# Attention, then routed experts: a 512-column copy ahead of two row copies, six row tiles, one weight load issued later

## The chip, the cores and the metric

The kernel runs on one core of one Trainium2 chip. The metric is device time in microseconds (us). Five engines work beside each other, each through its own instruction stream in order: PE (matrix products), DVE, ACT and POOL (element work), and SP, which here only issues DMA transfers. PE, DVE, ACT and POOL wait for each other and for transfers by semaphores.

## The reference

```python
scores = scale * np.matmul(q, k.transpose(0, 1, 3, 2))      # q, k, v: (8, 12, 448, 64)
scores = np.where(mask, -1000000000.0, scores)              # causal
attn = np.exp(scores - np.max(scores, axis=-1, keepdims=True))
attn = attn / (np.sum(attn, axis=-1, keepdims=True) + 1e-09)
x = np.matmul(attn, v)                                      # reordered to (3584, 768)
...
logits = x @ w_gate                                         # 8 experts
expert_idx = np.argmax(logits, axis=1)
gate_w = probs[np.arange(N), expert_idx]
for e in range(E):                                          # at most 80 tokens each, by largest gate_w
    h = np.maximum(x[tok_idx] @ w1[e], 0.0)                 # w1: (8, 768, 1024), w2: (8, 1024, 768)
    out[tok_idx] = gate_w[tok_idx, None] * (h @ w2[e])
```

Tokens that no expert keeps give rows of zeros.

## The kernel before

**Attention.** The eight batches go one after the other, each as six pairs of heads. Each pair passes through scores (PE), masked row minima (DVE), exponentials (ACT), transposes (PE) and products with v (PE). Between these stand, by a table of due times, the steps of the batch before: its gate, its choice of 80 tokens for each expert so far, and the writing of its rows of x to a DRAM buffer `xs`.

**The tail.** The last batch has nothing behind it to hide in. Its steps are issued in the order of a string of names, `TAIL` (L37 to L42), which a loop at the end of the manual schedule walks through. Each name issues one step, on the engine that the step uses. In a name `rNw` is the transpose of row group N by PE (L566) and `rNe` its scaling and its store: `ROW_ENGINES` gives r0 to DVE (L581), r1 to r3 to ACT (L576, one instruction per head), and r4 to r7 to ACT and POOL (a copy out of PSUM by ACT, L578, then a product in place by POOL, L579). Each `rNe` ends with a store of the row tile `xr` into `xs`, issued by SP (L582). Row groups 3 and 7 have 64 rows, the others 128.

**The choice.** `r0t` and `r1t` transpose two tables on PE (L676) and `r0c` and `r1c` copy them from PSUM into `ex` (L679): `r0c` on DVE the one-hot rows, `r1c` on ACT the three 16-bit parts of the gate weights. `rl`, `lt`, `cp`, `ro` compare the earlier batches' table with the new weights. `c3w` to `c0w` are products of the two halves of `ex` on PE (L690), `c3l` to `c0l` the comparisons on DVE (L693). From them come the ranks, the moves into the table (`rr`, `tn`, `tab`), and at the end `idx`, the rows of `xs` that each expert reads (L838). `*6`, `*2`, `*5` and `*18` issue that many products of no use (`wp`, L1010), which keep PE at work.

**The experts.** The first gather (L1098, on POOL, an indirect DMA) reads expert 0's rows out of `xs`. By its semaphores it waits for the landing of every row store and for `idx`. POOL then writes one column of a `wl` tile (L1228), for which DVE's first weight split (L1066) waits. Weights come as 32 pieces of 1536 KB, split by ACT (L1081) and DVE (L1066) into two 16-bit halves. There are ten buffers for pieces (`wraw`). Nine loads are issued before the tail's choice begins; the name `piece` in `TAIL` issues the tenth, into space that `close` frees. The eleventh has to wait until the first buffer is free again, which needs the splits.

Row tiles `xr` come from a pool with a fixed number of buffers in turn; a row group that takes a buffer waits until the store that last read it has landed. The loads and stores named here are all issued by SP, on one queue.

Of the kernel before, what the change touches and what calls it, by code (L numbers as in the profile page):

```python
# [7 lines left out]
F32 = mybir.dt.float32  # L8
# [9 lines left out]
P = 128  # L18
# [16 lines left out]
LATE = 23  # L35

TAIL = """  # L37
u ta ya rest rest tb yb v0 td yd tc yc v1 vy guard invert last_rows w gp0 wy close piece rest rest gp1 gs
r0w r0e lp r1w r1e r2w r3w r4w r5w *6 lg logit shifted chosen r2e r3e sums one_hot weight weighted columns parts
r0t r0c r1t rl lt r4e r5e r1c r6w r7w cp ro r6e c3w c3l r7e c2w c2l c1w c1l c0w c0l  # L40
*2 gt places earlier own *5 rank rr tn tab *18
"""  # L42
ROW_ENGINES = "vaaapppp"
# [3 lines left out]
def attention_then_moe(  # L47
# [32 lines left out]
    spool = sel_stack.enter_context(tc.tile_pool(name="sel", bufs=2, side="right"))  # L80
# [11 lines left out]
    def bank(shape, dtype, name):  # L92
        return (ps_x or ps_m).tile(shape, dtype, name=name, tag="x" if ps_x else "misc")
# [51 lines left out]
    def whole_tile(t):  # L145

        return slice(queries(t).start, queries(t).start + P)
# [329 lines left out]
    NH = NP // 2  # L477
# [29 lines left out]
    def norm_of(bt, t, hs, m):  # L507
        return bt.rl[0:m, hs] if t == NO else bt.sums[0:m, t * H + hs.start:t * H + hs.stop]
# [40 lines left out]
    def row_group(bt, t, g, how="v"):  # L549

        b = bt.b
        m = min(P, S - t * P)
        got = []

        def turn():
            if ps_x:

                own = len(row_banks) % 2
                tp = (ps_t if own else ps_m).tile([P, NH, P], F32, name="rt", tag="tp" if own else "misc",
                                                  padded_shape=[P, 4, P])  # L560
                row_banks.append(tp)
            else:
                tp = bank([P, NH, P], F32, "rt")
            got.append(tp)
            for i in range(NH):
                nc.tensor.transpose(tp[:, i, :], bt.xu[:, g * NH + i, whole_tile(t)], ident)  # L566

        def store():
            tp = got[0]
            xr = spool.tile([P, NH * P], F32, name="xr", tag="xr", bufs=4)  # L570
            src = tp[0:m].rearrange("k p (j d) -> k (p j) d", d=DH)
            dst = xr[0:m].rearrange("k (h d) -> k h d", d=DH)
            norm = norm_of(bt, t, slice(g * 2 * NH, (g + 1) * 2 * NH), m)
            if how == "a":
                for i in range(2 * NH):
                    nc.scalar.mul(dst[:, i, :], src[:, i, :], norm[:, i:i + 1])  # L576
            elif how == "p":
                nc.scalar.copy(dst, src)  # L578
                nc.gpsimd.tensor_tensor(out=dst, in0=dst, in1=norm.unsqueeze(2).to_broadcast([m, 2 * NH, DH]), op=ALU.mult)  # L579
            else:  # L580
                nc.vector.tensor_tensor(out=dst, in0=src, in1=norm.unsqueeze(2).to_broadcast([m, 2 * NH, DH]), op=ALU.mult)  # L581
            nc.sync.dma_start(xs[b * S + t * P:b * S + t * P + m, g * NH * P:(g + 1) * NH * P], xr[0:m, :])  # L582
        return [turn, store]
# [311 lines left out]
    with tc.manual_schedule():  # L895
# [79 lines left out]
        rest = [f for k in sorted(plan) for f in plan.pop(k)]  # L975
# [226 lines left out]
    for s in range(NSL):  # L1202
# [4 lines left out]
        for e in range(E):  # L1207
            u = Unit()
# [8 lines left out]
        with tc.manual_schedule(engines={mybir.EngineType.PE}):  # L1217
            for e in range(E + 1):
                if e < E:
                    u = units[e]  # L1220
# [70 lines left out]
```

## Time and profile before

| | us |
|---|---|
| median of 3 runs | 495.69 |
| lowest and highest | 493.9, 499.05 |
| the profiled execution's own time | 493.27 |
| its span, first to last instruction | 491.6 |
| mean granted clock of PE, share of full | 0.991 |

The span is 1.67 us shorter than the profiled execution's time, which holds the start and the end around it. The attention part fills about 0 to 344 us of the span, the tail of the last batch about 344 to 372 us and the experts the rest. A row of a timeline gives the start, the duration, the engine, the line and the tiles written and read; what stands in brackets is how long the engine was idle ahead of it and what ended the wait.

### The profile page before, as it was taken

How to read it: one execution, taken by the hardware profiler on the slowest of the kernel's cores; microseconds unless marked ns; L12 is line 12 of the kernel's file. 1: busy time of each engine (PE TensorE's matmuls, PEld its weight loads, DVE VectorE, ACT ScalarE, POOL GpSimd, SP SyncE). 2: the span in 40 equal slices, each digit the busy share in tenths (PEclk: the TensorE clock that was granted, in tenths of full speed). 3: DMA queues.
4: the chain of work that ended last, by engine and by line, in shares of the span. 5: the costliest groups of instructions: out<-in, count | busy, mean ns of one | idle time of the engine just before them, and what ended most of it. 6: DMA issues, size and time to landing. Idle time of an engine off the chain costs nothing. (4 is left out here: it accounts for less than half of the span.)

```text
span 491.6 us, 14840 instructions
## 1 busy us (share of the span) xinstructions
PE 447.9 (91%) x5282; PEld 343.1 (70%) x5282; DVE 427.8 (87%) x1297; ACT 419.4 (85%) x1089; POOL 270.6 (55%) x343
## 2 busy tenths in 40 slices
PE   3899989999999999999999999999979999989885
PEld 1566656756766675676667567677538999989885
DVE  5787879979988997998999799899568999999982
ACT  5999989979997997999799799988485999989881
POOL 6788786565668665566866556580136155511001
PEclk9999999999999999999999999999979999999999
DMA  7777996899579579856957985539936999999921
GB/s 217 198 186 190 275 274 189 249 264 285 148 214 269 147 231 253 259 148 215 262 153 227 270 240 157 187 119 328 418 137 201 372 387 387 391 423 424 421 81 41
DMA packets 49145, 120.88 MB, mean 246 GB/s; under 512 B 6146, under 2 KB 33026, under 8 KB 45616
## 3 DMA queue, kind: packets, MB, share of 16 engines
q1 hardware_dynamic: 47856, 116.21, 73.5%
q0 software_dynamic: 1056, 3.51, 2.3%
q8 instruction: 41, 0.67, 0.6%
q10 hardware_dynamic: 160, 0.23, 0.2%
q14 instruction: 32, 0.26, 0.2%
HBM read 96.36 MB, written 23.99 MB: 245 GB/s over the span
## 5 line engine op out<-in xcount | busy, mean ns | idle before, releaser
L421 ACT ACTIVATE prob<-ns,nb 128x128 f32<-128x128 f32 (+3 forms) x336 | 176.8, 528 | 20.5 <-DVE nb L418 19.0
L418 DVE CUSTOM_DVE_ANT_0 ns<-sp,mask 128x384 f32<-128x384 f32 (+2 forms) x288 | 116.2, 415 | 24.3 <-PE sp L397 10.7
L438 PE MATMUL tp<-ident,prob 128*128 128x128 f32 x768 | 121.5, 278 | 8.0 <-ACT prob L421 6.9
L438 PEld LDWEIGHTS tp<-ident,prob 128*128 128x128 f32 x768 | 88.5, 142 | 26.0 <-ACT prob L421 14.3
L1066 DVE SCALAR_TENSOR_TENSOR wl<-wraw,wh 128x768 f16<-128x768 f32 (+1 forms) x98 | 97.7, 1061 | 4.2 <-ACT wh L1081 2.4
L372 POOL TENSOR_TENSOR qk<-qk,qk 128x448 f16<-128x448 f32 x94 | 97.4, 1056 | 5.9 <-DVE qk L364 2.8
L450 ACT COPY PT<-tp 128x512 f32<-128x512 f32 x144 | 82.4, 572 | 16.3 <-PE sp L396 13.0
L367 POOL TENSOR_TENSOR qk<-qk,qk 64x448 f16<-64x448 f32 x47 | 49.3, 1049 | 81.3 <-ACT qk L360 45.2
L468 PE MATMUL xp<-PT,vt 128*64 128x448 f32 (+3 forms) x768 | 91.3, 380 | 0.0
L1081 ACT ACTIVATE wh<-wraw 128x768 f16<-128x768 f32 (+1 forms) x98 | 84.3, 924 | 2.4 <-PE hp L1141 1.7
L396 PE MATMUL sp<-qk 128*128 128x384 f16 (+2 forms) x288 | 75.9, 278 | 9.0 <-ACT qk L349 5.6
L468 PEld LDWEIGHTS xp<-PT,vt 128*64 128x64 f32 x768 | 54.9, 137 | 41.6 <-issue 22.4
L397 PE MATMUL sp<-qk 128*128 128x384 f16 (+2 forms) x288 | 78.0, 276 | 0.8 <-DVE qk L348 0.8
L1138 PEld LDWEIGHTS <-wh 128*128 128x128 f16 x668 | 67.2, 101 | 2.6 <-issue 2.6
L1140 PEld LDWEIGHTS <-wh 128*128 128x128 f16 x668 | 66.7, 100 | 2.0 <-issue 2.0
L1141 PEld LDWEIGHTS <-wl 128*128 128x128 f16 x668 | 66.7, 100 | 0.2 <-issue 0.2
L421 ACT ACTIVATION_READ_ACCUMULATOR prob<-ns,nb 128x1 f32 x336 | 63.8, 190 | 0.0
L1195 POOL DMA_INDIRECT out<-yo,idx x8 | 22.8, 2844 | 66.9 <-ACT yo L1192 61.8
L368 POOL TENSOR_TENSOR qk<-qk,qk 64x448 f16<-64x448 f32 x47 | 48.9, 1040 | 3.5
L1141 PE MATMUL op<-hh,wl 128*128 128x80 f16 x348 | 38.9, 202 | 1.3 <-issue 1.3
L396 PEld LDWEIGHTS <-qk 128*128 128x128 f16 x288 | 28.5, 99 | 15.8 <-issue 6.5
L1140 PE MATMUL op<-hl,wh 128*128 128x80 f16 x348 | 38.9, 202 | 0.6 <-issue 0.6
(173 smaller groups left out, 910.1 us busy)
## 6 DMA issues: line engine op xcount, KB each, us to landing
wraw<-w SPq DMA_DIRECT2D x27, 1536.0 KB, 15.6
qk<-k_t SPq DMA_DIRECT2D x92, 224.0 KB, 5.0
out<-mask_l SPq DMA_DIRECT2D x56, 192.0 KB, 3.9
qk<-q_t SPq DMA_DIRECT2D x23, 448.0 KB, 3.4
vt<-v_t SPq DMA_DIRECT2D x24, 384.0 KB, 5.8
xs<-xr SPq DMA_DIRECT2D x48, 192.0 KB, 3.3
wraw<-w SPq DMA_DIRECT2D x24, 256.0 KB, 5.6
vt<-v_t SPq DMA_DIRECT2D x24, 64.0 KB, 5.5
```

The lines of the kernel that those rows point to most:

```text
L372: nc.gpsimd.tensor_tensor(out=k_lo[j][:, i], in0=kf[j][:, i], in1=k_hi[j][:, i], op=ALU.subtract)
L396: nc.tensor.matmul(sp[:, 0:w], qx[:, p, t * P:w], kx[:, p, 0:w], start=True, stop=False)
L397: nc.tensor.matmul(sp[:, 0:w], qx[:, p, t * P:w], lx[:, p, 0:w], start=False, stop=True)
L418: pr.masked = nc.vector.tensor_tensor_reduce(out=ns[:, 0:w], in0=sp[:, 0:w], in1=m, scale=-1.0 / 8.0, scalar=HUGE, op0=ALU.add, op1=ALU.mi ...
L421: nc.scalar.activation(pr.P[:, off:off + w], ns[:, 0:w], AF.Exp, bias=nb, scale=-1.0, accum_out=total)
L438: nc.tensor.transpose(pr.tp[:, i], pr.P[:, off:off + P], ident)
L450: copy(dst, src)
L468: state["pe"] = nc.tensor.matmul(xp[rows, 0:w], st["vt"][:, c, p * P + j * DH:p * P + (j + 1) * DH], pr.PT[:, j, n0:n0 + w], start=(c == 0 ...
L1066: return nc.vector.scalar_tensor_tensor(out=l, in0=src, scalar=SW, in1=h, op0=ALU.mult, op1=ALU.subtract)
L1081: nc.scalar.activation(h, src, AF.Copy, scale=SW)
L1140: nc.tensor.matmul(o, wh[:, ws], al[:, c, :], start=False, stop=False, skip_group_check=True)
L1141: nc.tensor.matmul(o, wl[:, ws], ah[:, c, :], start=False, stop=(x == n - 1), skip_group_check=True)
```

## The change

Three things change. In `TAIL`, `r1c` moves from behind `r5e` to ahead of `r4e`, and `piece` moves from behind `close` to behind `r5e`. The row tiles `xr` get six buffers for four.

```diff
 TAIL = """
-u ta ya rest rest tb yb v0 td yd tc yc v1 vy guard invert last_rows w gp0 wy close piece rest rest gp1 gs
+u ta ya rest rest tb yb v0 td yd tc yc v1 vy guard invert last_rows w gp0 wy close rest rest gp1 gs
 r0w r0e lp r1w r1e r2w r3w r4w r5w *6 lg logit shifted chosen r2e r3e sums one_hot weight weighted columns parts
-r0t r0c r1t rl lt r4e r5e r1c r6w r7w cp ro r6e c3w c3l r7e c2w c2l c1w c1l c0w c0l
+r0t r0c r1t rl lt r1c r4e r5e piece r6w r7w cp ro r6e c3w c3l r7e c2w c2l c1w c1l c0w c0l
...
-            xr = spool.tile([P, NH * P], F32, name="xr", tag="xr", bufs=4)
+            xr = spool.tile([P, NH * P], F32, name="xr", tag="xr", bufs=6)
```

On ACT, in the tail, from r2e (L576) to the first split of weights (L1081), the difference of the two orders:

```order
 L576 ACTIVATE xr<-rt,sums 128x64 x6
 L576 ACTIVATE xr<-rt,rql 64x64 x6
-L578 COPY xr<-rt 128x384 x2
 L679 COPY ex<-selt 24x512
-L578 COPY xr<-rt 128x384
+L578 COPY xr<-rt 128x384 x3
 L578 COPY xr<-rt 64x384
 L1081 ACTIVATE wh<-wraw 128x1024 x8
```

The copy of the gate parts (L679) now stands directly behind r3e, and the copies of r4 to r7 (L578) follow it without a break.

On SP, from the last row store of the batch before to the loads of the experts part (`wraw<-w` is a weight piece, `xs<-xr` a row store, `out<-mask_l` a store of zeros):

```order
 L582 DMA xs<-xr 64x384
 L301 DMA out<-mask_l 128x384
-L196 DMA wraw<-w 128x3072 x2
+L196 DMA wraw<-w 128x3072
 L582 DMA xs<-xr 128x384 x3
 L582 DMA xs<-xr 64x384
-L582 DMA xs<-xr 128x384 x3
+L582 DMA xs<-xr 128x384 x2
+L196 DMA wraw<-w 128x3072
+L582 DMA xs<-xr 128x384
 L582 DMA xs<-xr 64x384
 L196 DMA wraw<-w 128x3072 x22
```

Of the two pieces that stood ahead of all eight row stores one stays; the other is now behind the stores of r0 to r5 and ahead of those of r6 and r7. On PE, DVE and POOL the order is the same.

## Rows read from the trace of the kernel before

**Rows 1.** The page's head: the span, and each engine's busy time.

```profile
span 491.6 us, 14840 instructions
...
PE 447.9 (91%) x5282; PEld 343.1 (70%) x5282; DVE 427.8 (87%) x1297; ACT 419.4 (85%) x1089; POOL 270.6 (55%) x343
```

**Rows 2.** Windows: stretch, length, busy (PE, PEld, DVE, ACT, POOL), clock, DMA, GB/s.

```profile
364.00:370.00 6.00, 5.68 (x35) 2.88 (x36) 3.09 (x15) 6.00 (x7) 1.37 (x4) 0.50 0.16 50
...
430.00:440.00 10.00, 8.57 (x203) 8.34 (x200) 10.00 (x14) 8.06 (x14) 2.28 (x1) 1.00 1.01 424
```

**Rows 3.** Timeline of POOL: start, length, engine, line, operation [idle before <- releaser].

```profile
360.96 2.40 POOL L579 TENSOR_TENSOR xr<-xr,sums 128x384 f32<-128x384 f32 x3 [4.02 <-ACT xr L578]
...
368.58 1.08 POOL L1098 DMA_INDIRECT xg<-xs,idx  x1 [4.44 <-DVE gws L843]
369.68 0.11 POOL L1228 MEMSET wl<- 128x1 f16 x1
```

**Rows 4.** Timeline of DVE, from the rank counts to the first expert.

```profile
359.84 0.22 DVE L724 TENSOR_SCALAR ro<-cp,pnum 80x8 f16<-80x8 f32 x1 [0.29 <-PE cp L719]
362.28 0.75 DVE L693 SCALAR_TENSOR_TENSOR less<-rn,ggw,before 128x512 bf16<-128x512 f32 x1 [2.22 <-PE rn L690]
...
367.61 0.16 DVE L838 TENSOR_TENSOR idx<-xf,tn 80x8 int32<-80x8 f32 x1
...
369.82 3.50 DVE L1066 SCALAR_TENSOR_TENSOR wl<-wraw,wh 128x1024 f16<-128x1024 f32 x3 [1.57 <-POOL wl L1228]
...
380.02 0.66 DVE L1117 SCALAR_TENSOR_TENSOR xl<-xtp,xh 128x480 f16<-128x480 f32 x1
```

**Rows 5.** Timeline of ACT around the copy of the gate parts.

```profile
356.99 1.31 ACT L576 ACTIVATE xr<-rt,rql 64x64 f32<-64x64 f32 x6
360.41 0.94 ACT L578 COPY xr<-rt 128x384 f32<-128x384 f32 x2 [2.10 <-DMA xs<-xr]
361.25 0.57 ACT L679 COPY ex<-selt 24x512 bf16<-24x512 bf16 x1
```

**Rows 6.** Timeline of PE, from the keep-warm products to the first expert.

```profile
355.78 1.30 PE L1010 MATMUL wp<-before,identb 128*128 128x448 bf16 x6
...
357.98 0.38 PE L676 MATMUL selt<-identb,mv 128*128 128x128 bf16 x4 [0.34 <-DVE mv L665]
...
359.05 0.75 PE L719 MATMUL cp<-oh,lt 128*80 128x8 bf16 x4
361.87 0.65 PE L690 MATMUL rn<-ex 128*128 128x512 bf16 x3 [2.07 <-ACT ex L679]
...
367.23 5.04 PE L1010 MATMUL wp<-before,identb 128*128 128x448 bf16 x18
372.11 0.58 PE L1112 MATMUL xtp<-ident,xg 80*128 80x80 f32 x6
...
378.62 0.58 PE L1112 MATMUL xtp<-ident,xg 80*128 80x80 f32 x6
```

**Rows 7.** Timeline of SP's DMA queue, the whole stretch.

```profile
344.36 4.24 SPq L196 DMA_DIRECT2D wraw<-w  x2
353.52 11.10 SPq L582 DMA_DIRECT2D xs<-xr  x8
373.34 0.34 SPq L196 DMA_DIRECT2D wraw<-w  x1
```

**Rows 8.** DMA issues (KB, us to landing): pieces nine, ten, r0, r4, piece eleven.

```profile
wraw<-w SPq DMA_DIRECT2D x1, 1536.0 KB, 11.8
...
wraw<-w SPq DMA_DIRECT2D x1, 1536.0 KB, 11.5
...
xs<-xr SPq DMA_DIRECT2D x1, 192.0 KB, 6.8
...
xs<-xr SPq DMA_DIRECT2D x1, 192.0 KB, 1.9
...
wraw<-w SPq DMA_DIRECT2D x1, 1536.0 KB, 9.8
```

## The prediction

> **What bounds the kernel now.** Read the page first [rows 1]: PE, DVE and ACT are each busy over 85% of the span, which is an average over stages and decides nothing here. The windows tell the stages apart [rows 2]: while the experts run, DVE is busy 10.00 of 10.00 us and the DMA engines 1.01 of their time, so that part is full and moves as a block with its start; at 364 to 370 us PE is granted half its clock and DVE is busy 3.09 of 6.00 us, so the tail waits. Then the timelines, backwards from the experts. DVE's first weight split starts at 369.82 [rows 4], released by a memset that POOL issues right behind the first gather, and the gather starts at 368.58 after 4.44 us of waiting [rows 3]. It needs `idx`, which DVE ends at 367.61 + 0.16 = 367.77 [rows 4], and the landing of all row stores. SP's last store is issued by 353.52 + 11.10 = 364.62 [rows 7] and one such store lands in 1.9 [rows 8], so by 366.5: today `idx` is the later one, and the gather follows its end by 0.81.
>
> `idx` in turn hangs on a stop. PE has done the second table's transposes at 357.98 + 0.38 = 358.36 [rows 6], but ACT copies them into `ex` only at 361.25 [rows 5]: ahead of that copy stand r4e and r5e, and r4e waits 2.10 us for the landing of a row store, r0's, whose tile it takes with four buffers. PE then stands idle 2.07 us until `ex` [rows 6], and DVE waits 2.22 us for PE [rows 4].
>
> **Term 1, the copy ahead of the row groups.** ACT is free at 356.99 + 1.31 = 358.30 and the transposes end at 358.36, so the copy of 0.57 runs at about 358.4 and ends at 359.0 [rows 5, 6]. The products of L690 stand on PE behind `cp`, which ends at 359.80 for want of DVE's earlier work, so they start there, 2.07 earlier than 361.87 [rows 6]. DVE's first comparison follows the products' start by 362.28 - 361.87 = 0.41 and `ro`, which ends at 360.06: it starts at 360.2, 2.1 earlier [rows 4, 6]. All steps from there to `idx` are a chain of DVE and PE with nothing else in it, so `idx` ends at 365.7, and by `idx` alone the gather would start at 366.5. PE would also lose the idle time ahead of its fall to half clock, which I put at nothing on this chain, since its products there are short.
>
> **Term 2, six row tiles.** With six, r4e and r5e take tiles of older batches and wait for nothing; r6e and r7e take those of r0 and r1. The 2.10 wait [rows 5] goes. Two copies by ACT take 0.94 [rows 5], so r4 to r7 are copied from 358.9 to 360.8 and the splits of weights behind them start earlier by some 2 (358.4 for 360.41), which is worth nothing by itself: DVE's splits wait for POOL, not for them [rows 4]. POOL's product starts 360.96 - 360.41 = 0.55 behind ACT's copy and takes 2.40 / 3 = 0.80 [rows 3, 5]: r4 ends at 360.25, r5 at 361.05, r6 at 361.85, r7 at 362.65. Without term 3, all would have landed at 362.7 + 1.9 = 364.6, ahead of `idx`. In exchange r6e waits for r0's store. That one lands today at 353.52 + 6.8 = 360.3 [rows 7, 8], behind the tenth piece; with that piece gone from there it is 3.6 earlier (next term), so r6e at 359.8 finds it done.
>
> **Term 3, the tenth piece behind r5.** What a piece does to stores behind it is in the DMA issues. Piece nine is issued at 344.36 and lands in 11.8, at 356.2. Piece ten's issue ends at 344.36 + 4.24 = 348.60, and an issue takes 0.34, so it starts at 348.26 and lands in 11.5, at 359.8: 3.6 behind the other [rows 7, 8]. r0, issued at 353.52, lands at 360.3, 0.5 behind piece ten, although a store alone takes 1.9 [rows 8]. SP's transfers land in the order of their issue. So 3.6 is what a piece costs the stores behind it.
>
> Now the piece is issued when r5's store is: 361.05, and 0.34 later, say 361.4. Only r6 and r7 are behind it, but the gather needs both. The piece's landing is bounded by rows. Lowest: stores pass it, and it costs nothing. Highest: piece eleven, whose issue also finds its queue empty but meets the gathers, takes 9.8 [rows 8]. I take the stores' own time less the 0.5 that it adds behind another, 1.9 - 0.5 = 1.4, plus 3.6: 5.0, because at 361.4 nothing else but row stores is under way. The piece lands at 366.4, r6 at 366.9, r7 with half the rows at 367.2. The gather starts, with the same 0.81, at 368.0 and not at 366.5. Against 368.58 that leaves 0.6 of the 2.1.
>
> The piece itself is not missed: it is the last of ten loads and is read by the second layer of the second expert, after all of the first expert's work; DVE has not reached the second expert's input at 380.02 [rows 4]. SP's queue has nothing behind r7 until 373.34 [rows 7].
>
> [...]
>
> **Sum.** 0.6 less at the start of the experts; nothing before it is on the path, and behind it DVE and DMA are full [rows 2], so it passes to the end: 493.27 - 0.6 = 492.7 for the profiled execution. That one stands 2.4 under the median of 495.69, so the median goes to **495.1**. The bounds of the piece give gather starts from 366.5 (a gain of 2.1: 493.6) to 361.4 + 9.8 + 0.8 for r6 and r7 + 0.81 = 372.8 (a loss of 4.2: 499.9).
>
> **Rivals.**
>
> *The piece costs the stores nothing*, since it comes into an empty queue and the stores are small. Then `idx` ends last and all of 2.1 stays: 493.6. For it: row stores of today land in 1.9 beside nothing. Against it: r0's 6.8 [rows 8]. Chance 0.2.
>
> *Slower: PE stands still ahead of the first expert and its clock falls on that expert's first layer.* Today 18 products of no use bridge the time to the gather; they take 5.04, because PE has only half its clock for most of it, and the expert's first transposes follow at 372.11 without a gap [rows 6]. At full clock six take 1.30, so 18 take 3.9 [rows 6]; starting 2.1 earlier, at 365.1, they end at 369.0. The transposes need the gather, which today is 372.11 - 368.58 = 3.5 ahead of them at most, so with the gather at 368.0 they may stand at 371.5: an idle time of up to 2.5. The one of 2.07 at 359.80 [rows 6] is followed by the half clock of 364 to 370 [rows 2]. Six us at half clock cost PE 3.0. In the first layer that moves the second expert's transposes from 378.62 to 378.62 - 0.6 + 3.0 = 381.0; DVE's step on them today starts at 380.02 without idle time noted [rows 4, 6], so DVE would stand 2.4 later than now: 498.1. It decides once the gather, and not the end of the 18 products, releases PE, after a stop like the one of 2.07. Against it: 3.5 is an upper bound, and the layer's products begin right behind.
>
> [...] Chance 0.2.
>
> *The piece lands as late as piece eleven does today*: 499.9, chance 0.05.
>
> *Nothing changes*, because r6e or some other wait still holds ACT, or the gather comes out where it was: 495.7. Chance 0.1.
>
> My forecast has 0.45.
>
> **Range and chances.** The forecast's own range is 494 to 496. To hold 8 in 10 the range must take in the full gain, 493.6, and the slower rival, 498.1, with the median of a few runs uncertain by about 1 (they lie from 493.9 to 499.05): **492.6 to 498.6**. A measurement here can tell about 1% from no change, that is 490.7 and 500.6. Even the full gain of 2.1 is 0.4%, so faster by more than 1% has 0.04; slower by more than 1% takes the late piece together with the fallen clock, 0.05; the rest, 0.91, is within 1%.
>
> **What would show it.** Term 1: ACT's copy at 358.4, PE's products at about 359.8, DVE's first comparison at 360.2, `idx` at 365.7. Term 2: no wait for a row store ahead of r4e, and r7's product done at 362.7. Term 3: the stores of r6 and r7 issued at about 362 and 362.7 landing 4 to 5 us later, and POOL's gather released by a transfer and not by DVE. If the gather starts at 366.5 the first rival is right; if the granted clock stands at half after 370 the second. The forecast is wrong if the gather moves by other than 0 to 1.2, or if the experts' part does not move with the gather.

## The result and the profile after

The changed kernel takes 501.48 us (median of 4 runs, 500.27 to 503.6) against 495.24 for the kernel before (493.9 to 499.05): a ratio of 1.0126, 95% interval [1.0081, 1.017]. It is slower, and lies above the range of 492.6 to 498.6. The profiled execution took 503.6, with a span of 501.8 and a mean granted clock of 0.977, against 491.6 and 0.991 before. The two profiled executions stand at opposite ends of their runs: their spans are 10.2 apart, the medians 6.2, so a difference between the two traces is larger than the typical one.

ACT and DVE move as the first two terms say. ACT's timeline (columns as in [rows 5]):

```profile
358.21 0.57 ACT L679 COPY ex<-selt 24x512 bf16<-24x512 bf16 x1
358.69 1.58 ACT L578 COPY xr<-rt 128x384 f32<-128x384 f32 x4
```

The copy of the gate parts starts at 358.21, not 361.25, and the copies of r4 to r7 follow without a wait. On DVE, the lines that answer to [rows 4]:

```profile
359.88 0.75 DVE L693 SCALAR_TENSOR_TENSOR less<-rn,ggw,before 128x512 bf16<-128x512 f32 x1
...
365.33 0.16 DVE L838 TENSOR_TENSOR idx<-xf,tn 80x8 int32<-80x8 f32 x1
...
371.24 3.50 DVE L1066 SCALAR_TENSOR_TENSOR wl<-wraw,wh 128x1024 f16<-128x1024 f32 x3 [5.27 <-POOL wl L1228]
...
386.97 0.66 DVE L1117 SCALAR_TENSOR_TENSOR xl<-xtp,xh 128x480 f16<-128x480 f32 x1 [5.39 <-ACT xh L1116]
```

`idx` is 2.28 earlier than before, but DVE's first split is 1.42 later and its step on the second expert 6.95 later. Between them stands the gather. POOL's timeline, as in [rows 3]:

```profile
359.23 2.40 POOL L579 TENSOR_TENSOR xr<-xr,sums 128x384 f32<-128x384 f32 x3 [2.48 <-ACT xr L578]
...
370.00 1.08 POOL L1098 DMA_INDIRECT xg<-xs,idx  x1 [7.59 <-issue]
```

The gather starts 4.51 us after `idx` ended at 365.49: DVE no longer releases it. SP's queue, as in [rows 7], and two of its issues, as in [rows 8], the piece and r6:

```profile
353.34 7.85 SPq L582 DMA_DIRECT2D xs<-xr  x6
361.29 0.38 SPq L196 DMA_DIRECT2D wraw<-w  x1
361.76 1.13 SPq L582 DMA_DIRECT2D xs<-xr  x2
```

```profile
wraw<-w SPq DMA_DIRECT2D x1, 1536.0 KB, 6.9
...
xs<-xr SPq DMA_DIRECT2D x1, 192.0 KB, 7.0
```

The piece lands at 361.29 + 6.9 = 368.2 and r6, issued at 361.76, at 368.8; the gather needs r7, behind both. On PE, as in [rows 6]:

```profile
359.47 0.72 PE L690 MATMUL rn<-ex 128*128 128x512 bf16 x3
...
364.95 3.56 PE L1010 MATMUL wp<-before,identb 128*128 128x448 bf16 x18
373.26 1.03 PE L1112 MATMUL xtp<-ident,xg 80*128 80x80 f32 x6 [4.75 <-DMA xg<-xs,idx]
374.81 10.53 PE L1131 MATMUL hp<-xw,wraw 128*128 128x80 f32 x48 [0.51 <-ACT xw L1115]
385.13 1.01 PE L1112 MATMUL xtp<-ident,xg 80*128 80x80 f32 x6
```

The 18 products of no use, now at a granted clock of 1.00, end at 368.51. PE then stands 4.75 us until the gathered rows are there. The windows, columns as in [rows 2], show what follows:

```profile
364.00:368.50 4.50, 4.04 (x30) 2.15 (x30) 1.15 (x6) 3.85 (x5) 0.00 (x0) 1.00 0.84 316
368.52:373.26 4.74, 0.00 (x0) 0.03 (x1) 2.02 (x2) 0.00 (x0) 3.06 (x3) 0.98 0.04 8
373.26:390.10 16.84, 16.33 (x123) 16.09 (x124) 10.20 (x11) 6.09 (x10) 4.95 (x4) 0.50 0.90 300
390.20:400.00 9.80, 9.80 (x237) 9.80 (x235) 9.36 (x11) 9.62 (x15) 0.00 (x0) 1.00 0.78 285
489.20:492.50 3.30, 3.30 (x55) 3.30 (x52) 0.03 (x1) 0.20 (x1) 0.91 (x1) 0.50 0.29 79
```

The granted clock is 0.50 from the first transposes of the first expert to 390.1, against 1.00 from 364 to 368.5 and from 390.2 to 400. The first layer's 48 products take 10.53. In the kernel before, at a granted clock of 1.00 from 373.19 to 378.77, they take 5.58:

```profile
373.19 5.58 PE L1131 MATMUL hp<-xw,wraw 128*128 128x80 f32 x48 [0.51 <-ACT xw L1115]
```

The second expert's transposes stand at 385.13, against 378.62 [rows 6]. A second stretch at 0.50 with PE busy, 489.2 to 492.5, lies in the last expert; the kernel before has 1.00 from 470 to 489.4. How much longer the last expert takes can be read from DVE's step on the last expert's input, in the kernel before, the changed kernel and the third experiment below, in this order:

```profile
463.38 0.65 DVE L1117 SCALAR_TENSOR_TENSOR xl<-xtp,xh 128x480 f16<-128x480 f32 x1
471.70 0.65 DVE L1117 SCALAR_TENSOR_TENSOR xl<-xtp,xh 128x480 f16<-128x480 f32 x1
466.02 0.65 DVE L1117 SCALAR_TENSOR_TENSOR xl<-xtp,xh 128x480 f16<-128x480 f32 x1
```

From there to the end of the span it is 28.2 before, and 30.1 and 30.0 in the two others: 1.9 of the 10.2. The mean clock of the third experiment's profiled execution, 0.994 over 496.0 us, makes 6 us at half clock, an estimate, as many as the 30.1 of the changed kernel hold at their mean of 0.90; its first layers had 1.00 (373.9 to 400).

### The profile page after: what moved, and what is told of

Its sections match the earlier page's. It is cut to its first block, busy times and chain, and to the rows that moved or that the text cites. A ratio compares the mean times of both kernels' runs of the same rounds, so it can differ in the third digit from the quotient of the medians.

```text
span 501.8 us, 14841 instructions
## 1 busy us (share of the span) xinstructions
PE 453.9 (90%) x5282; PEld 351.0 (70%) x5282; DVE 428.0 (85%) x1297; ACT 419.4 (84%) x1089; POOL 269.7 (54%) x343
## 5 line engine op out<-in xcount | busy, mean ns | idle before, releaser
L1081 ACT ACTIVATE wh<-wraw 128x768 f16<-128x768 f32 (+1 forms) x98 | 84.4, 924 | 4.2 <-PE hp L1141 1.8
L1141 PEld LDWEIGHTS <-wl 128*128 128x128 f16 x668 | 68.4, 102 | 3.7 <-issue 3.7
L1138 PEld LDWEIGHTS <-wh 128*128 128x128 f16 x668 | 68.9, 103 | 1.9 <-issue 1.9
L1140 PEld LDWEIGHTS <-wh 128*128 128x128 f16 x668 | 68.5, 102 | 0.1
L1140 PE MATMUL op<-hl,wh 128*128 128x80 f16 x348 | 40.5, 205 | 1.6 <-issue 1.6
L1138 PE MATMUL op<-hh,wh 128*128 128x80 f16 x348 | 40.5, 205 | 0.6 <-issue 0.6
L1141 PE MATMUL op<-hh,wl 128*128 128x80 f16 x348 | 40.5, 205 | 0.0
```

Of the source, the lines that this page charges most:

```text
L1081: nc.scalar.activation(h, src, AF.Copy, scale=SW)
L1138: nc.tensor.matmul(o, wh[:, ws], ah[:, c, :], start=(x == 0 and i % per == 0), stop=False, skip_group_check=True)
L1140: nc.tensor.matmul(o, wh[:, ws], al[:, c, :], start=False, stop=False, skip_group_check=True)
L1141: nc.tensor.matmul(o, wl[:, ws], ah[:, c, :], start=False, stop=(x == n - 1), skip_group_check=True)
```

## The experiments

Theory A: the piece holds r6 and r7 back, so the gather is late, PE stops ahead of the first expert and its clock falls on the first layers. Theory B: the late gather alone costs, and the clock only shows it. Theory C: the copy or the tiles hurt in themselves. Every ratio is to the kernel before, timed beside each; the medians below are of 6 to 12 runs. Each cut of code is the difference from a kernel that is named ahead of it; dots stand for names or lines left out.

**The piece back at its old place** (from the changed kernel)

```diff
-... w gp0 wy close rest rest gp1 gs
+... w gp0 wy close piece rest rest gp1 gs
-... lt r1c r4e r5e piece r6w
+... lt r1c r4e r5e r6w
```

> The change without its third part: the tenth piece stands ahead of all row stores again, copy first and six tiles stay. Theory A (the piece keeps r6 and r7 from landing, PE waits for the gather and its clock falls): r7 lands by 365, the gather starts at about 366.2 on idx, PE stops for under 1 us ahead of the first expert, the clock stays full, 493.0 us. Theory B (the late gather alone costs, whatever the clock): also about 493. Theory C (the copy first or the six tiles hurt, by ACT's earlier splits or otherwise): 499 or more.

492.78 us, ratio 0.9938 [0.9907, 0.9968]: faster than the kernel before. Theory C falls. Its gather on POOL, and its first layer on PE:

```profile
367.70 1.08 POOL L1098 DMA_INDIRECT xg<-xs,idx  x1 [3.49 <-DVE gws L843]
```

```profile
366.35 5.27 PE L1010 MATMUL wp<-before,identb 128*128 128x448 bf16 x18
371.46 0.58 PE L1112 MATMUL xtp<-ident,xg 80*128 80x80 f32 x6
372.55 5.58 PE L1131 MATMUL hp<-xw,wraw 128*128 128x80 f32 x48 [0.51 <-ACT xw L1115]
```

The gather is released by DVE again, PE does not stop and the layer takes 5.58. The gather was 1.5 later than I expected, since the tail began 0.6 later in this execution than in the changed kernel's and the clock fell within it (0.51 from 364 to 370), as it does before; the 18 products took that up.

**The piece alone moved** (from the kernel before)

```diff
-... wy close piece rest rest
+... wy close rest rest
-... r4e r5e r1c r6w
+... r4e r5e r1c piece r6w
```

> The third part alone: four tiles, the copy of the gate parts behind r5e as before, the tenth piece behind that copy. Theory A: r4e no longer waits, since r0's store has nothing ahead of it, but r6 and r7 land at about 369, the gather starts near 370, PE stops for some 4 us and runs the first layer at half clock: 500 to 502 us. Theory C: under 497, since neither the copy nor the tiles are changed.

500.83 us, ratio 1.0114 [1.0073, 1.0155], as slow as the whole change. POOL and PE:

```profile
369.36 1.08 POOL L1098 DMA_INDIRECT xg<-xs,idx  x1 [7.53 <-DMA xs<-xr]
```

```profile
372.62 0.64 PE L1112 MATMUL xtp<-ident,xg 80*128 80x80 f32 x6 [4.53 <-DMA xg<-xs,idx]
373.76 10.53 PE L1131 MATMUL hp<-xw,wraw 128*128 128x80 f32 x48 [0.51 <-ACT xw L1115]
```

Here the profile names the row store as the gather's releaser. The third part is the cause of the slowdown, alone and with the rest. Its copies and `idx`, on ACT and DVE:

```profile
358.07 0.88 ACT L578 COPY xr<-rt 128x384 f32<-128x384 f32 x2
```

```profile
364.91 0.16 DVE L838 TENSOR_TENSOR idx<-xf,tn 80x8 int32<-80x8 f32 x1
```

With four tiles and the old order of the copies, r4e does not wait for r0's store, and `idx` stands as early as in the whole change (365.33). So with the piece moved, the gain at `idx` needs neither of the first two parts: it was the piece ahead of r0's store that kept r4e waiting.

**The whole change with PE kept at work until the gather** (from the changed kernel)

```diff
-*2 gt places earlier own *5 rank rr tn tab *18
+*2 gt places earlier own *5 rank rr tn tab *43
```

> The whole change, with 43 products of no use for 18 ahead of the first expert, which at 0.187 us each reach from 365.0 to about 373.1, where the gather lands. Theory A: the gather still starts at 370.0, but the clock stays full, the first layer takes 5.6 us and not 10.5, and only the gather's 1.4 us remain: 496.7 us. Theory B: the gather's lateness is what costs, 501 to 502 us as with the whole change.

497.9 us, ratio 1.0058 [1.0032, 1.0084]. POOL and PE:

```profile
370.78 1.08 POOL L1098 DMA_INDIRECT xg<-xs,idx  x1 [7.66 <-issue]
```

```profile
365.65 8.29 PE L1010 MATMUL wp<-before,identb 128*128 128x448 bf16 x43
373.89 0.61 PE L1112 MATMUL xtp<-ident,xg 80*128 80x80 f32 x6
375.01 5.58 PE L1131 MATMUL hp<-xw,wraw 128*128 128x80 f32 x48 [0.51 <-ACT xw L1115]
```

The gather starts 0.8 later still than in the whole change, but the clock stays at 1.00 (373.9 to 400) and the layer takes 5.58. 1.0126 became 1.0058: in the medians the fallen clock on the first layers is about half of the loss against before. Theory B falls. It is 1.2 above my 496.7, though. The trace has two reasons: the gather is 2.2 later than before and not 1.4, and the last expert takes 1.8 more than before here too.

**The copy alone, and the tiles alone** (each from the kernel before)

```diff
-... lt r4e r5e r1c r6w
+... lt r1c r4e r5e r6w
```

```diff
-xr = spool.tile([P, NH * P], F32, name="xr", tag="xr", bufs=4)
+xr = spool.tile([P, NH * P], F32, name="xr", tag="xr", bufs=6)
```

> The first part alone: the copy of the gate parts ahead of r4e and r5e, four tiles, the piece at its old place. Theory A: idx at about 365.4, r4e still waits for r0's store until 360.3, so r7 lands at about 366.2 and the gather starts at 367.1: 493.8 us, if PE's stop of some 1.7 us leaves the clock up. Theory C with the copy as its cause: 499 or more.

> The second part alone: six row tiles, the copy of the gate parts behind r5e, the piece at its old place. Theory A: r4e and r5e wait for nothing and end at about 359.3, the copy ends at 359.9, where PE gets through with cp anyway, so idx and the gather come as with copy and tiles together: 493 us, the same as the kernel with both parts. If the order of the copy matters beside the tiles, 1 us or more above that.

493.99 us, ratio 0.9982 [0.9953, 1.0011], and 494.35, ratio 0.9986 [0.9948, 1.0025]: neither can be told from no change. With the copy alone ACT waits for r0's store as expected, now behind the copy:

```profile
358.42 0.57 ACT L679 COPY ex<-selt 24x512 bf16<-24x512 bf16 x1
359.95 1.83 ACT L578 COPY xr<-rt 128x384 f32<-128x384 f32 x4 [0.95 <-DMA xs<-xr]
```

PE stops for 1.22 ahead of the first expert:

```profile
370.66 0.61 PE L1112 MATMUL xtp<-ident,xg 80*128 80x80 f32 x6 [1.22 <-DMA xg<-xs,idx]
```

With the tiles alone the profiled execution shows something else, on PE:

```profile
370.89 0.64 PE L1112 MATMUL xtp<-ident,xg 80*128 80x80 f32 x6 [1.06 <-DMA xg<-xs,idx]
372.04 10.45 PE L1131 MATMUL hp<-xw,wraw 128*128 128x80 f32 x48 [0.51 <-ACT xw L1115]
```

After a stop of 1.06 ahead of the first expert the layer took 10.45 here, with a mean clock of 0.979 for the execution; after one of 1.22 with the copy alone it took 5.58, with 0.997. The runs of the tiles alone reach from 492.13 to 499.45. Whether copy and tiles are worth more together than either stays open.

**No products of no use ahead of the first expert** (from the first experiment)

```diff
-... rank rr tn tab *18
+... rank rr tn tab
```

> Copy first, six tiles, the piece at its old place, and the last 18 products of no use left out, so that PE stands idle some 4 to 5 us ahead of the first expert with a gather that is not late (about 367.7). Theory A: the clock falls on the first layer, 3 to 5 us above the same kernel with the 18: 496 to 498 us. Theory B: the clock's fall costs little, 493 to 494.

499.13 us, ratio 1.0063 [1.0034, 1.0093], above my 496 to 498. POOL and PE:

```profile
367.20 1.08 POOL L1098 DMA_INDIRECT xg<-xs,idx  x1 [4.22 <-DVE gws L843]
```

```profile
370.54 1.03 PE L1112 MATMUL xtp<-ident,xg 80*128 80x80 f32 x6 [4.55 <-DMA xg<-xs,idx]
372.09 10.53 PE L1131 MATMUL hp<-xw,wraw 128*128 128x80 f32 x48 [0.51 <-ACT xw L1115]
```

The granted clock is 0.50 from 370.6 to 386.6. Same code as the first experiment but for those 18, a gather no later, and first transposes that are 0.9 earlier: 0.9938 against 1.0063, about 6 us for the clock alone. Timed beside it, the kernel with 24 products at this place (the last experiment) has 0.997, by which it is 4.6. The rival had this price at 2.4.

**The piece behind all row stores** (from the changed kernel)

```diff
-... r5e piece r6w r7w cp ro r6e c3w c3l r7e c2w
+... r5e r6w r7w cp ro r6e c3w c3l r7e piece c2w
```

> Copy first, six tiles, the piece behind the stores of all row groups. Theory A: no store is behind the piece, the gather starts on idx at about 366.5; the piece is under way until about 369 and shares the DMA engines with the gather's rows: 493 to 495 us. If a transfer of another queue waits as long behind the piece as a store of the same queue does, the first rows come at 372 and PE's clock falls: 497 to 500.

494.79 us, ratio 0.9984 [0.9953, 1.0016]: the slowdown is gone. POOL's gather, and its time to landing:

```profile
367.19 1.08 POOL L1098 DMA_INDIRECT xg<-xs,idx  x1 [4.22 <-DVE gws L843]
```

```profile
xg<-xs,idx POOLq DMA_INDIRECT x1, 3.5
```

Beside the piece the gather lands in 3.5, against 3.0 with the piece at its old place (the first experiment, whose 0.9938 is lower; the two intervals just overlap).

**The piece on ACT's queue** (from the changed kernel)

```diff
-            nc.sync.dma_start(t, src)
+            (eng or nc.sync).dma_start(t, src)
...
-                load_piece()
+                load_piece(eng=nc.scalar)
```

> The whole change, with the tenth piece issued by ACT on its own queue, at the same place, so that r6 and r7 have no piece ahead of them on SP's. Theory A in the form that it is the order on one queue: r6 and r7 land at about 366, the gather starts at 367 to 367.5, PE's stop is under 2 us: 493 to 496 us. If the piece takes the DMA engines from the stores whatever the queue, they land at 368 to 369 as before and it is 500 to 502 us.

499.87 us, ratio 1.0085 [1.0045, 1.0125]. The issues in order, the piece, r4, r5 and r6:

```profile
wraw<-w ACTq DMA_DIRECT2D x1, 1536.0 KB, 7.8
...
xs<-xr SPq DMA_DIRECT2D x1, 192.0 KB, 6.4
...
xs<-xr SPq DMA_DIRECT2D x1, 192.0 KB, 6.1
...
xs<-xr SPq DMA_DIRECT2D x1, 192.0 KB, 5.8
```

The piece is on another queue, issued at 359.44, ahead of r4, and r4 to r6 still wait for it. What each queue moved shows how, first from 362 to 365, then from 366 to 367 (q10 is ACT's queue, q1 is SP's; behind each stand its transfers, their MB and their time as a share of 16 engines):

```profile
q10 hardware_dynamic: 80, 0.98, 105.7%
```

```profile
q1 hardware_dynamic: 222, 0.31, 84.2%
q10 hardware_dynamic: 16, 0.05, 12.2%
```

Between 362 and 365 SP's queue moved nothing, although r4 and r5 were issued by 362.1. So it is not the order on SP's queue alone that holds the stores: in these windows the DMA engines moved the piece first, 0.98 MB of it from 362 to 365, and 0.31 MB on SP's queue from 366 to 367. What decides between the two queues is not shown. In the profiled execution PE stops for 3.21 ahead of the first expert and the first layer takes 10.53, at a granted clock of 0.50 (372.9 to 389). Two of the 12 runs, with a mean clock of 0.990 and 0.989, took 493.77 and 494.2, the ten others, at 0.978 to 0.986, 498.96 to 501.7. That points to PE's clock for most of the difference with the piece at the same place, but there is no trace of those two runs.

**More products of no use, with the piece at its old place** (from the first experiment)

```diff
-*2 gt places earlier own *5 rank rr tn tab *18
+*5 gt places earlier own *11 rank rr tn tab *24
```

> Copy first, six tiles, the piece at its old place, 24 products of no use for 18 ahead of the first expert, so that they reach the gather also where the clock stays full through the tail. Theory A: no run has PE idle for more than 0.5 us there: 492.3 us, and at most 1 us below the kernel with 18.

> Copy first, six tiles, the piece at its old place, and more products of no use in the tail: 5 for 2, 11 for 5, 24 for 18. If it is the clock that scatters the runs of this kernel (492 where the granted clock is 0.997 or above, 495 and more where it is 0.991 and below), these keep it up: a mean clock of 0.995 or above in nearly all runs and 492 us, 1 us below the same kernel without them and with less scatter. If the products get in the way of the tail's own, idx comes later and it is 493 or more.

Only the last number changed (24 for 18): 494.42 us, ratio 0.997 [0.9937, 1.0003], above what I expected and not told from no change. All three numbers changed: 492.5 us, 491.76 to 494.28, ratio 0.9961 [0.9933, 0.9988], faster than the kernel before. Its windows:

```profile
360.00:370.00 10.00, 9.39 (x70) 4.90 (x68) 7.46 (x23) 8.01 (x10) 5.60 (x7) 1.00 0.22 73
370.00:380.00 10.00, 9.49 (x155) 9.34 (x153) 9.83 (x11) 6.92 (x12) 4.75 (x3) 1.00 0.91 290
```

The clock is 1.00 from 360 to 380, where [rows 2] had 0.50, and the mean clock of its 12 runs is 0.993 to 0.999. It and the first experiment are the versions that beat both kernels; I cannot tell the two apart.

## Why the prediction was wrong

**Term 1 and term 2 held in their numbers, though term 3 gives the same gain.** The copy came at 358.21 (358.4 expected), PE's products at 359.47 (359.8), DVE's comparison at 359.88 (360.2), `idx` ended at 365.49 (365.7); POOL's last row product ended at 359.23 + 4 x 0.8 = 362.4 (362.65). The 2.1 us at `idx` are there. But term 3 removes the same wait: with the piece alone moved `idx` is as early, so in the whole change the gain cannot be put down to the first two parts. With the piece at its old place and both parts, 0.6, 0.3 and 0.4% less time was measured (the first experiment and the two with more products; the middle one is not told from no change). The first of these, 3 us, is more than 2.1, and its profiled execution, with a gather 0.9 earlier than before and a span of 491.8, does not show where it comes from.

**Term 3 was mis-sized.** I put the piece's landing at 5.0 after its issue, an estimate from 1.4 of a store's 1.9 and the 3.6 between two pieces; it took 6.9. The 3.6 was read where the next piece follows in a full queue. With no other piece under way it needed longer: the window from 364 to 368.5 of the changed kernel has 316 GB/s, against 424 in [rows 2]; why the rate is lower is not shown. The gather then started 370.00 and not 368.0, 1.4 later than before instead of 0.6 earlier. That alone turns the sign of the forecast's 0.6: in the third experiment, with the clock at 1.00, DVE's step on the second expert stands at 381.84 against 380.02 [rows 4], and the ratio is 1.0058.

**The step that failed most is the choice of the forecast over its slower rival.** The sum let "0.6 less at the start of the experts" pass to the end, and the stop of PE was given a chance of 0.2, with the remark that 3.5 from gather to transposes is an upper bound. My own numbers had a stop of up to 2.5 there, more than the one of 2.07 that stands ahead of the half clock of [rows 2]. It was 4.75. From gather to transposes it took 373.26 - 370.00 = 3.26, close to the bound, so by these numbers, an estimate, even the forecast's gather at 368.0 would have left a stop of some 2.7. The late piece and the fallen clock were also kept apart as two rivals, although the first brings the second: slower by more than 1%, which takes both, had a chance of 0.05, and that is what came. And the rival's price, 2.4, took the fall from [rows 2], 6 us long, as its length. In the first layers it lasted 17 us and put DVE's step on the second expert back by 6.95. The kernel without the 18 products prices it at 4.6 to about 6 us by itself.

**Of the reasons, one was half right.** "SP's transfers land in the order of their issue" described r0's wait, but on ACT's queue the piece held the stores as well. The rival that the piece costs nothing was wrong. That the piece's late load is not missed by the experts is not contradicted: with the piece behind all stores the time cannot be told from the kernel before, but it is 0.5% above the first experiment, with intervals that just overlap.

**What stays open.** Lateness and clock do not add: from 0.9938, the late gather without the fall on the first layers gives 1.0058, the fall without the late gather 1.0063, both 1.0126. Part of this may be the last expert, 1.9 and 1.8 longer than before in the changed kernel and the third experiment. Without the products it is likely longer too, an estimate: from the first transposes of the first expert to the end of the span, the profiled execution takes 499.0 - 370.54 = 128.5 there and 501.8 - 373.26 = 128.5 in the changed kernel. Then a sum counts it twice. What brings it, and whether it is in all their runs, is not shown.

## What to carry to other kernels

A large load that is put where no other load is under way can still delay the small transfers that the next stage waits for: here r6, issued behind the piece, landed in 7.0 us and not the 1.9 of a store alone. Put it behind the last of those (a ratio of 0.9984 here, against 1.0126) or ahead of them all (0.9938), and read its landing where it finds the queue as it will be (6.9 here, and 3.6 behind another piece). Let products that keep PE at work reach the moment at which the next real product can start: with 43 the first layer took 5.58 here, with 18, which ended 4.75 us ahead of that moment, 10.53. A change that makes the chain ahead of them faster also makes them start earlier (364.95 for 367.23 here), so their number belongs to the change. And where the work behind a stop is bound by PE, as the first layers here, price the stop by the layer behind it at the lower clock (10.53 for 5.58 here), not by the stop.

## What the hardware showed that I had not expected

- Behind a load on ACT's queue, a store on SP's landed 6.4 us after its issue, nearly as late as behind the same load on SP's own queue (7.0), against 1.9 without a load. SP's queue moved nothing from 362 to 365 while ACT's did.
- A 1536 KB load took 6.9 us to land with no other piece under way, while of two in a row the second landed 3.6 behind the first.
- After a stop of 1.06 us in one execution the first layer took 10.45 us, and after one of 1.22 in another 5.58. In the changed kernel the clock, once down, stayed at 0.50 for 17 us although PE was busy 16.33 of 16.84 us.
- The profiled execution of the changed kernel has a further stretch at 0.50 in the last expert, from 489.2 to 492.5, with PE busy 3.30 of 3.30 us. From DVE's step on that expert's input to the end of the span it took 30.1 us, against 28.2 before, where the clock was 1.00 from 470 to 489.4.
